# Folding a feature map into projection weights in 64 by 64 tiles on two PSUM banks, with later row statistics held back

## The chip, the core and the metric

The kernel runs on one core of a Trainium2 chip. The metric is the device time of one execution in microseconds (us); the engines are named as in the profile: PE (TensorE, the matrix engine), PEld (its weight loads), DVE (VectorE), ACT (ScalarE), POOL (GpSimd) and SP (SyncE, which issues the DMAs).

## What is computed

Two layers, each an attention block with a learned feature map and a dense block with the Mish activation, over x of 2048 rows by 640 columns, in float32, 32 heads of 20 columns:

```
def _A_ref(x, wqkv, w_phi, wo):
    q, k, v = split into heads of (x @ wqkv)                  # 32 heads, 20 wide
    pq = einsum("bhsd,hdf->bhsf", q, w_phi)                   # a 20 x 20 map for each head
    pk = einsum("bhsd,hdf->bhsf", k, w_phi)
    phi_q = concat([softmax(pq), softmax(-pq)], axis=-1)      # 40 wide
    phi_k = concat([softmax(pk), softmax(-pk)], axis=-1)
    kv, z = phi_k^T v, sum of phi_k over the rows
    o = (phi_q kv) / (phi_q z + 1e-6)
    return o @ wo
def _B_ref(x, w1, b1, w2):
    h = x @ w1 + b1
    return (h * tanh(softplus(h))) @ w2
for _ in range(2):
    x = x + _A_ref(layernorm(x), ...)
    x = x + _B_ref(layernorm(x), ...)
```

## The kernel before

The 2048 rows are worked through in eight blocks of 256 (two tiles of 128). Every large matmul is done in three parts for precision: each operand is split into a high part (rounded to the fp32r format, an ACT copy) and a low part (what is left, a DVE or POOL subtraction), and high x high, high x low and low x high are added up in PSUM.

`w_phi` isn't applied to q and k. Before the first projection it is multiplied into the query and key columns of `wqkv` ("folded"): the weights come in transposed (`wqk_t`), in raw tiles of rows of that transpose, and a matmul of a raw tile (stationary, 128 columns for one k, the index of 128 input features of 640) with the block-diagonal `phi_bd` (moving) gives folded weights for some heads, straight in the layout that the projections use. Of each head's 20 outputs only 19 are made: `shift_phi` (POOL) first subtracts the last column from the others, since a softmax doesn't change when its input is shifted, so there are 608 folded columns. `fold_part` issues one matmul, `fold_end` evicts a finished part from PSUM into a high part (ACT, L275) and a low part (DVE, L276).

Before the change the raw tiles t = 0 to 3 hold 120 rows (6 heads), and t = 4 and 5 hold 80 (4 heads). For each k there are six matmuls, three into one bank (342 columns) and three into another (266 columns), and two evictions.

The first stage of layer 0 (`attend_first` with `first is None`) is written in an order of its own (`with written()`): loads of x, `phi_bd` and the raw tiles; the first block's layer-norm statistics (L295, L297, L304, L305, L307); the query weights' fold of t = 0 to 2 for all k (`pcs`), with the first normalized rows and their transposition (L325, L331) in between; half of the first query projection (`q0[0]`, L391); then for each k the rest of the query fold and `make_v(k - 1)`, which splits one piece of the value weights (L142 on ACT, L143 on DVE); then the other half `q0[1]`. Everything behind it, the key weights' fold (`fold_phi(kv_ws, ...)`), the other projections, `features` (L407 to L427: the two softmaxes of a query or key tile `r` or `big`: copy out of PSUM, L416 maximum and minimum, L417 and L419 subtractions, exponential, L425 row sums, L426 reciprocal, L427 product; L472 turns a query tile around) and the statistics of the next blocks (`fetch_normed`), is put in order by a scheduler which works with its own time estimates: each engine gets a fixed list of instructions and works through it strictly in order, waiting on semaphores. All DMAs here are issued by SP, also in a fixed order, with at most eight outstanding. The folded query and key weights are stored to DRAM for the second layer (L222, L223).

PSUM has eight banks here: two tiles `mm` of two banks each, and four tiles `one` of one bank. The x tiles have two buffers, so that a block's x is loaded (L432) when the block two before it has been normalized (L134, `xn`).

Of the kernel before, what the change touches and what calls it, by code (L numbers as in the profile page):

```python
# [8 lines left out]
F32 = mybir.dt.float32  # L9
F32R = mybir.dt.float32r  # L10
AF = mybir.ActivationFunctionType
ALU = mybir.AluOpType
# [4 lines left out]
P = 128  # L17
S = 2048
D = 640
F = 1536  # L20
H = 32
DH = 20
DL = DH - 1
KD = D // P
KF = F // P
BT = 2
# [5 lines left out]
QK = H * DL  # L32
# [12 lines left out]
def kernel(  # L45
# [13 lines left out]
    nc = tc.nc  # L59
# [3 lines left out]
    wts = ctx.enter_context(tc.tile_pool(name="wts", bufs=1))  # L63
# [50 lines left out]
    x1_d = dram.tile([S, D], F32, name="x1_d")  # L114
    x2_d = dram.tile([S, D], F32, name="x2_d")

    last_act, in_written, last_low, last_load = [None], [False], [None], [None]

    @contextmanager
    def written():  # L120
# [19 lines left out]

    def split(hi, lo, st):
        nc.scalar.activation(hi, st, AF.Copy)  # L142
        nc.vector.tensor_tensor(lo, st, hi.bitcast(F32), op=ALU.subtract)  # L143

    def r1_spare(tag):
        return wts.tile([P, F], F32, tag=tag, name="raw1")
# [26 lines left out]
    def r2_wide(j, dtype=F32R):  # L173
        return wts.tile([P, 2, D], dtype, tag=f"r2{j}", name=f"r2{j}")
# [66 lines left out]
    def load_raw(which, ts=range(6)):  # L241

        raw = []
        for t in ts:
            rows = 120 if t < 4 else 80
            if t < 5:
                r = wts.tile([P, D], F32, tag=f"r2{'hl'[which]}{5 + t}", name=f"raw{which}{t}")
            else:
                r = r2_wide(10 + which, F32)[:, 0]

            n = P if t < 5 else rows
            c0 = which * D + (t * 120 if t < 5 else D - rows)
            nc.sync.dma_start(r[:n], wqk_t[c0:c0 + n, :])
            raw.append((r, rows))
        return raw

    def fold_part(ps, k, t, bd, raw):

        r, rows = raw[t]
        heads = rows // DH  # L260
        n = DL * (6 * (t % 3) if t < 5 else 10)
        nc.tensor.matmul(ps[:, n:n + heads * DL].rearrange("p (j d) -> p j d", d=DL), r[:rows, k * P:(k + 1) * P],
                         bd[:rows, t, :rows].rearrange("p (j d) -> p j d", d=DH)[:, :, :DL], start=True, stop=True)

    def shift_phi(bd, ts):

        b = bd[:, ts].rearrange("p t (j d) -> p (t j) d", d=DH) if isinstance(ts, slice) else (
            bd[:80, ts, :80].rearrange("p (j d) -> p j d", d=DH))
        nc.gpsimd.tensor_tensor(b[:, :, :DL], b[:, :, :DL], b[:, :, DL:].to_broadcast([b.shape[0], b.shape[1], DL]),
                                op=ALU.subtract)  # L270

    def fold_end(ws, ps, k, c):
        n0, n1 = (0, 18 * DL) if c == 0 else (18 * DL, QK)
        hi, lo = ws[k][0][:, n0:n1], ws[k][1][:, n0:n1]
        nc.scalar.activation(hi, ps[:, :n1 - n0], AF.Copy)  # L275
        nc.vector.tensor_tensor(lo, ps[:, :n1 - n0], hi.bitcast(F32), op=ALU.subtract)  # L276

    def fold_phi(ws, bd, raw):

        pss = {}  # L280
        for k, c in ((0, 0), (1, 0), (2, 0), (3, 0), (0, 1), (1, 1), (2, 1), (3, 1), (4, 0), (4, 1)):
            if c == 0:
                mm = None if k % 2 else mm_tile()
                pss[k] = [one_tile(), one_tile()] if k % 2 else [mm[:, 0], mm[:, 1]]
            ps = pss[k][c]
            for t in range(3 * c, 3 * c + 3):
                fold_part(ps, k, t, bd, raw)
            fold_end(ws, ps, k, c)


    def norm_stats(t, xt):

        bn = work.tile([P, 2, 6], F32, tag="bn", name="bn", bufs=2)
        for c in range(2):
            nc.vector.bn_stats(bn[:, c], xt[:, t, c * HC:(c + 1) * HC])  # L295
        mv = work.tile([P, 2], F32, tag="mv", name="mv", bufs=3)
        nc.vector.bn_aggr(mv, bn)  # L297
# [137 lines left out]
    def attend_first(layer, x_src, first):  # L435


        def fetch_normed(b):
            if layer:
                return load_turned(n2_d[b], [row_tile] * 3, nc.gpsimd)  # L440
            xt = fetch(x_src, b) if b > 1 else early
            norm_scale(b, [norm_stats(t, xt) for t in range(BT)])
            return xt

        pending = []
# [48 lines left out]
        if first is None:  # L494
            with written():
                xt = fetch(x_src, 0)
                bd = big_tile()[:120, :720].rearrange("p (t c) -> p t c", t=6)
                nc.sync.dma_start(bd[:, :3], phi_bd[:, :3])
                raw_q = load_raw(0, range(3))

                nc.vector.memset(bd[:80, 5, :80], 0.0)
                nc.sync.dma_start(bd[:40, 5, :40], phi_bd[80:120, 4, 80:120])
                nc.sync.dma_start(bd[40:80, 5, 40:80], phi_bd[:40, 5, :40])
                nc.sync.dma_start(bd[:, 3:5], phi_bd[:, 3:5])
# [8 lines left out]
                shift_phi(bd, slice(3, 5))  # L513
                shift_phi(bd, 5)

                q_ws = [r2_pair(k) for k in range(KD)]
                mm = [mm_tile(), mm_tile()]
                pcs = [mm[0][:, 0], mm[0][:, 1], mm[1][:, 0], mm[1][:, 1], one_tile()]
                for t in range(3):
                    for k in range(KD - 1):  # L520
                        fold_part(pcs[k], k, t, bd, raw_q)
                fold_end(q_ws, pcs[0], 0, 0)
# [4 lines left out]
                fold_end(q_ws, pcs[1], 1, 0)  # L527
                fold_end(q_ws, pcs[2], 2, 0)
                nxt = Transposed(xn)
                nxt.step()  # L530
                fold_end(q_ws, pcs[3], 3, 0)
                nxt.step()
                for t in range(3):
                    fold_part(pcs[4], 4, t, bd, raw_q)
                nxt.step()
                fold_end(q_ws, pcs[4], 4, 0)
# [474 lines left out]
```

## Time and profile before

| | us |
|---|---|
| median of 3 runs | 1365.76 |
| lowest and highest of them | 1362.42, 1367.02 |
| profiled execution, its own time | 1364.93 |
| span of that execution in the profile | 1363.0 |
| PE busy in it | 1351.1 (99%) |
| DVE, ACT, POOL busy | 1057.4, 574.7, 463.9 |

The profile is of one execution. In rows of the timeline the columns are start, duration, engine, line of the kernel, operation, output tile <- input tiles, partitions x elements, count, and in brackets the idle time of the engine ahead of it with what ended that. In rows of windows each engine has its busy time and in brackets the number of instructions; PEclk is the TensorE clock that was granted, as a share of full speed. A matmul in float32 stands as two rows (two passes) in the trace. Line numbers are those of the kernel before, also where the changed kernel is spoken of.

### The profile page before, as it was taken

Reading aid. Unit: us, or ns where it says so; the run is one execution under the profiler, and the core shown is the slowest. Engines: PE = TensorE matmul, PEld = TensorE weight load, DVE = VectorE, ACT = ScalarE, POOL = GpSimd, SP = SyncE. Lnnn points to the kernel's source line nnn. Section 1 sums busy time; section 2 is a strip of 40 time slices with the busy share of each in tenths; the row PEclk is TensorE's granted clock in tenths of the full one; section 3 lists DMA queues with packets and bytes.
Section 4 is the critical chain, followed back from the end, with each engine's and each line's share of the span. In section 5 each row is a group of like instructions: output and inputs, shape, how many; then the busy total and the mean of one; then the engine's idle time right before and its main releaser. Section 6 shows DMA issues by size and latency. Waiting matters only on the chain.

```text
span 1363.0 us, 30965 instructions
## 1 busy us (share of the span) xinstructions
PE 1351.1 (99%) x12896; PEld 1339.1 (98%) x12896; DVE 1057.4 (78%) x1801; ACT 574.7 (42%) x965; POOL 463.9 (34%) x417
## 2 busy tenths in 40 slices
PE   9999999999999999999999999999999999999998
PEld 9999999999999999999999999999999999999998
DVE  5888988876687887778769788788668777676775
ACT  4444344322454545445443334332236444444443
POOL 2355544444222222222226556634251211111111
PEclk9999999999999999999999999999999999999999
DMA  9543443798714442334463534468964221233200
GB/s 340 155 101 80 96 99 78 206 278 280 222 39 98 116 117 69 62 104 109 140 205 83 116 79 97 91 153 249 282 250 130 78 77 31 88 97 97 73 25 20
DMA packets 352629, 174.11 MB, mean 128 GB/s; under 512 B 287449, under 2 KB 324041, under 8 KB 352489
## 3 DMA queue, kind: packets, MB, share of 16 engines
q1 hardware_dynamic: 352489, 172.14, 46.3%
q8 instruction: 101, 1.65, 0.5%
q14 instruction: 39, 0.32, 0.1%
HBM read 106.23 MB, written 65.86 MB: 126 GB/s over the span
## 4 chain that ended last, share of the span: by engine, by line
PE 90%; DVE 3%; POOL 2%; DMA 1%; ACT 1%; issue 1%; SPq 0%; DVEq 0%; POOLq 0%; ACTq 0%
PE mm L839 25%; PE one L797 25%; PE mm L391 24%; PE one L391 10%; PE mm L675 2%; PE one L325 2%; PE one L464 1%; DMA raw<-in_w 1%; POOL big L427 1%; DVE r L425 1%; DVE m L416 1%; DVE r L419 1%; POOL r1l L164 1%; DVE big L417 0%; DMA e_d<-r 0%
## 5 line engine op out<-in xcount | busy, mean ns | idle before, releaser
L839 PE MATMUL mm<-r2h,ol 128*128 128x320 f32 x1280 | 304.9, 309 | 0.0
L823 POOL TENSOR_TENSOR ol<-big,ol 128x512 fp32r<-128x512 f32 (+1 forms) x98 | 131.0, 1337 | 477.8 <-ACT ol L822 419.6
L797 PE MATMUL one<-xtl,r1h 128*128 128x256 f32 x960 | 268.2, 279 | 0.0
L797 PE MATMUL one<-xth,r1l 128*128 128x256 f32 x960 | 268.0, 279 | 0.0
L797 PE MATMUL one<-xth,r1h 128*128 128x256 f32 x960 | 265.8, 279 | 0.0
L839 PEld LDWEIGHTS mm<-r2h,ol 128*128 128x128 f32 x1280 | 219.2, 188 | 0.0
L839 PE MATMUL mm<-r2l,ol 128*128 128x320 f32 x640 | 197.3, 309 | 0.0
L391 PE MATMUL mm<-r1h,xth 128*128 128x304 f32 (+1 forms) x600 | 185.2, 309 | 0.0
L391 PE MATMUL mm<-r1l,xth 128*128 128x304 f32 (+1 forms) x600 | 183.8, 306 | 0.0
L391 PE MATMUL mm<-r1h,xtl 128*128 128x304 f32 (+1 forms) x600 | 183.5, 306 | 0.2 <-POOL xtl L331 0.2
L797 PEld LDWEIGHTS one<-xtl,r1h 128*128 128x128 f32 x960 | 180.5, 188 | 0.0
L797 PEld LDWEIGHTS one<-xth,r1l 128*128 128x128 f32 x960 | 180.4, 188 | 0.0
L797 PEld LDWEIGHTS one<-xth,r1h 128*128 128x128 f32 x960 | 179.6, 188 | 0.0
L812 DVE TENSOR_SCALAR big<-big 128x512 f32<-128x512 f32 (+1 forms) x98 | 56.9, 581 | 110.3 <-ACT big L810 110.1
L839 PEld LDWEIGHTS mm<-r2l,ol 128*128 128x128 f32 x640 | 120.2, 188 | 0.0
L814 ACT ACTIVATE big<-big,two 128x512 f32<-128x512 f32 (+1 forms) x98 | 70.1, 715 | 116.2 <-DVE big L813 116.1
L822 ACT ACTIVATE ol<-big 128x512 fp32r<-128x512 f32 (+1 forms) x98 | 60.9, 622 | 137.8 <-DVE big L821 137.7
L810 ACT ACTIVATE big<-one,b1s 128x256 f32<-128x256 f32 x192 | 80.8, 467 | 89.0 <-PE one L797 88.4
L427 POOL TENSOR_TENSOR r<-r,r 128x1280 f32<-128x1280 f32 x32 | 77.2, 2411 | 117.3 <-DVE r L426 104.8
L391 PEld LDWEIGHTS mm<-r1h,xth 128*128 128x128 f32 x600 | 112.8, 188 | 1.1 <-DVE r1l L276 0.2
L391 PEld LDWEIGHTS mm<-r1h,xtl 128*128 128x128 f32 x600 | 112.8, 188 | 0.4 <-POOL xtl L331 0.4
L391 PEld LDWEIGHTS mm<-r1l,xth 128*128 128x128 f32 x600 | 112.8, 188 | 0.1
(141 smaller groups left out, 3118.7 us busy)
## 6 DMA issues: line engine op xcount, KB each, us to landing
e_d<-r SPq DMA_DIRECT2D x128, 160.0 KB, 4.0
big<-e_d SPq DMA_DIRECT2D x32, 640.0 KB, 7.1
x_d<-xt SPq DMA_DIRECT2D x23, 640.0 KB, 3.9
xt<-x_d SPq DMA_DIRECT2D x22, 640.0 KB, 5.3
n_d<-xn SPq DMA_DIRECT2D x168, 80.0 KB, 2.3
xt<-in_x SPq DMA_DIRECT2D x16, 640.0 KB, 4.6
xn<-x_d SPq DMA_DIRECT2D x28, 320.0 KB, 4.3
v<-n_d SPq DMA_DIRECT2D x30, 256.0 KB, 3.1
```

Source lines behind the costliest of these rows:

```text
L164: low.tensor_tensor(w[1][:, cs], st, w[0][:, cs].bitcast(F32), op=ALU.subtract)
L325: nc.tensor.transpose(ps[:, c, t * P:(t + 1) * P], self.rows[t][:, (c0 + c) * P:(c0 + c + 1) * P], ident)
L391: nc.tensor.matmul(ps[:, :w], a[:, sl], r, start=(k == 0 and n == 0), stop=(k == KD - 1 and n == 2))
L427: nc.gpsimd.tensor_tensor(eg, eg, r.unsqueeze(2).to_broadcast([P, 2 * H, DH]), op=ALU.mult)
L675: nc.tensor.matmul(po[64 * q:64 * q + 64, c, GW * j:GW * j + w], phs[g][:n, s0:s0 + 64], kvb[:n, g, :w], start=True, stop=True)
L797: nc.tensor.matmul(ph[:, j, :], l, r, start=(n == 0), stop=(n == 3 * KD - 1))
L810: exps[0] = nc.scalar.activation(part(ta, 0)[:, j - js.start], ph[:, j, :], AF.Exp, bias=b1s[:, 2 * pr + j:2 * pr + j + 1]).ins
L812: nc.vector.tensor_scalar_min(e, e, E_CAP)
L814: nc.scalar.activation(r, n, AF.Ln, bias=two)
L822: nc.scalar.activation(ah[:, js], n, AF.Copy)
L823: nc.gpsimd.tensor_tensor(al[:, js], n, ah[:, js].bitcast(F32), op=ALU.subtract)
L839: nc.tensor.matmul(pys[t][:, c, :HC], l[:, j, sl], r, start=(f == 0 and n == 0), stop=(f == KF - 1 and n == 2))
```

## The change

The raw tiles overlap: each holds 124 rows of which two stretches of 60 (3 heads each) begin at partitions 4 and 64; tile 0 of the query weights gets 4 rows of zeros ahead, and t = 5 is 64 rows with 2 heads. All of `phi_bd` comes in three transfers into a zeroed tile. A fold matmul now takes 64 rows (60 of them with heads) and 64 stationary columns and gives 57 columns (3 heads; 38 for t = 5): four for each tile and k, rows 0 to 63 into one bank (`ps[0]`), rows 64 to 123 into another (`ps[1]`), each in two column halves. `pair_banks` gives the two banks, either two tiles `one` or one tile `mm`. `fold_end` evicts a pair of banks in one instruction where it is one `mm` tile, in two where it is two `one` tiles, and the 38 columns of t = 5 in an instruction of their own. `fold_phi` works through k one after the other with all of t, in place of two halves. The statistics of the later blocks in layer 0 are issued no sooner than the last `split` (`issue_after(last_split[0])`).

```
     def split(hi, lo, st):
         nc.scalar.activation(hi, st, AF.Copy)
-        nc.vector.tensor_tensor(lo, st, hi.bitcast(F32), op=ALU.subtract)
+        last_split[0] = nc.vector.tensor_tensor(lo, st, hi.bitcast(F32), op=ALU.subtract).ins
...
+    def load_phi(bd):
+        nc.vector.memset(bd, 0.0)
+        for s in range(2):
+            nc.sync.dma_start(bd[4 + 60 * s:64 + 60 * s, :5], phi_bd[60 * s:60 * s + 60, :5, 60 * s:60 * s + 60])
+        nc.sync.dma_start(bd[24:64, 5, :40], phi_bd[:40, 5, :40])
...
+    def pair_banks(single):
+        if single:
+            return [one_tile(), one_tile()]
+        mm = mm_tile()
+        return [mm[:, 0], mm[:, 1], mm]
+
+    def fold_part(ps, k, t, t0, bd, raw):
+        n = 3 * (t - t0) * DL
+        heads = 3 if t < 5 else 2
+        for s in range(2 if t < 5 else 1):
+            rows = slice(64 * s, 64 if s == 0 else 124)
+            rhs = bd[rows, t, :heads * DH].rearrange("p (j d) -> p j d", d=DH)[:, :, :DL]
+            for q in range(2):
+                nc.tensor.matmul(ps[s][64 * q:64 * q + 64, n:n + heads * DL].rearrange("p (j d) -> p j d", d=DL),
+                                 raw[t][rows, k * P + 64 * q:k * P + 64 * q + 64], rhs, start=True, stop=True)
+
+    def fold_end(ws, ps, k, t0, t1):
+        n = min(t1, 5) - t0
+        w = 3 * DL
+        c0 = 2 * t0 * w
...
+        srcs = ([ps[2][:, :, :n * w].rearrange("p s (t d) -> p s t d", t=n)] if len(ps) > 2 else
+                [p[:, :n * w].rearrange("p (t d) -> p t d", t=n) for p in ps])
+        outs = list(zip(srcs, parts(ws[k][0]), parts(ws[k][1])))
+        if t1 > 5:
+            outs.append((ps[0][:, n * w:n * w + 2 * DL], ws[k][0][:, 10 * w:QK], ws[k][1][:, 10 * w:QK]))
+        for src, hi, lo in outs:
+            nc.scalar.activation(hi, src, AF.Copy)
+            nc.vector.tensor_tensor(lo, src, hi.bitcast(F32), op=ALU.subtract)
 
     def fold_phi(ws, bd, raw):
-        pss = {}
-        for k, c in ((0, 0), (1, 0), (2, 0), (3, 0), (0, 1), (1, 1), (2, 1), (3, 1), (4, 0), (4, 1)):
...
+        for k in range(KD):
+            ps = pair_banks(k % 2)
+            for t in range(6):
+                fold_part(ps, k, t, 0, bd, raw)
+            fold_end(ws, ps, k, 0, 6)
...
             xt = fetch(x_src, b) if b > 1 else early
-            norm_scale(b, [norm_stats(t, xt) for t in range(BT)])
+            with tc.issue_after(last_split[0]):
+                norm_scale(b, [norm_stats(t, xt) for t in range(BT)])
             return xt
...
                 q_ws = [r2_pair(k) for k in range(KD)]
-                mm = [mm_tile(), mm_tile()]
-                pcs = [mm[0][:, 0], mm[0][:, 1], mm[1][:, 0], mm[1][:, 1], one_tile()]
+                pcs = [pair_banks(k < 2) for k in range(KD - 1)]
...
                 for k in range(KD):
-                    ps = one_tile()
+                    ps = pair_banks(k % 2 == 0)
                     for t in range(3, 6):
-                        fold_part(ps, k, t, bd, raw_q)
-                    fold_end(q_ws, ps, k, 1)
+                        fold_part(ps, k, t, 3, bd, raw_q)
+                    fold_end(q_ws, ps, k, 3, 6)
                     if k > 0:
                         make_v(k - 1)
```

More of the change, by code (lines that the diff above doesn't have):

```diff
@@ L115 @@
     x2_d = dram.tile([S, D], F32, name="x2_d")
-    last_act, in_written, last_low, last_load = [None], [False], [None], [None]
+    last_act, in_written, last_low, last_load, last_split = [None], [False], [None], [None], [None]
     @contextmanager
@@ L244, in load_raw @@
         for t in ts:
[L245 to L254, printed above, removed]
-        return raw
[L257 to L263, printed above, removed]
+            r = (wts.tile([P, D], F32, tag=f"r2{'hl'[which]}{5 + t}", name=f"raw{which}{t}") if t < 5 else
+                 r2_wide(10 + which, F32)[:, 0])
@@ new lines, in load_raw @@
+            p0 = 4 if which == t == 0 else 0
+            n = P if t < 5 else 64
+            c0 = which * D + (120 * t - 4 if t < 5 else D - 64)
+            if p0:
+                nc.vector.memset(r[:p0], 0.0)
+            nc.sync.dma_start(r[p0:n], wqk_t[c0 + p0:c0 + n, :])
+            raw.append(r)
+        return raw
+    def load_phi(bd):
[3 more added lines that the diff above has]
+        nc.sync.dma_start(bd[24:64, 5, :40], phi_bd[:40, 5, :40])
@@ L265, in shift_phi @@
     def shift_phi(bd, ts):
[L267 to L269 removed]
+        b = bd[:, ts].rearrange("p t (j d) -> p (t j) d", d=DH)
+        nc.gpsimd.tensor_tensor(b[:, :, :DL], b[:, :, :DL], b[:, :, DL:].to_broadcast([P, b.shape[1], DL]),
                                 op=ALU.subtract)
[L272 to L276, printed above, removed]
@@ L278, in fold_phi @@
-    def fold_phi(ws, bd, raw):
-        pss = {}
-        for k, c in ((0, 0), (1, 0), (2, 0), (3, 0), (0, 1), (1, 1), (2, 1), (3, 1), (4, 0), (4, 1)):
[L282 to L288, printed above, removed]
+    def pair_banks(single):
[3 more added lines that the diff above has]
+        return [mm[:, 0], mm[:, 1], mm]
@@ new lines, in fold_end, with parts @@
+    def fold_end(ws, ps, k, t0, t1):
+        n = min(t1, 5) - t0
+        w = 3 * DL
+        c0 = 2 * t0 * w
+        def parts(x):
+            x = x[:, c0:c0 + 2 * n * w].rearrange("p (t s d) -> p s t d", t=n, s=2)
+            return [x] if len(ps) > 2 else [x[:, 0], x[:, 1]]
+        srcs = ([ps[2][:, :, :n * w].rearrange("p s (t d) -> p s t d", t=n)] if len(ps) > 2 else
[6 more added lines that the diff above has]
+            nc.vector.tensor_tensor(lo, src, hi.bitcast(F32), op=ALU.subtract)
@@ L496, in attend_first @@
                 xt = fetch(x_src, 0)
-                bd = big_tile()[:120, :720].rearrange("p (t c) -> p t c", t=6)
-                nc.sync.dma_start(bd[:, :3], phi_bd[:, :3])
+                bd = big_tile()[:, :360].rearrange("p (t c) -> p t c", t=6)
+                load_phi(bd)
                 raw_q = load_raw(0, range(3))
[L501 to L504, printed above, removed]
                 shift_phi(bd, slice(0, 3))
@@ L512, in attend_first @@
                 norm_scale(0, mvs)
-                shift_phi(bd, slice(3, 5))
-                shift_phi(bd, 5)
+                shift_phi(bd, slice(3, 6))
                 q_ws = [r2_pair(k) for k in range(KD)]
-                mm = [mm_tile(), mm_tile()]
-                pcs = [mm[0][:, 0], mm[0][:, 1], mm[1][:, 0], mm[1][:, 1], one_tile()]
+                pcs = [pair_banks(k < 2) for k in range(KD - 1)]
                 for t in range(3):
                     for k in range(KD - 1):
-                        fold_part(pcs[k], k, t, bd, raw_q)
-                fold_end(q_ws, pcs[0], 0, 0)
+                        fold_part(pcs[k], k, t, 0, bd, raw_q)
+                fold_end(q_ws, pcs[0], 0, 0, 3)
                 xn = [row_tile() for _ in range(BT)]
@@ L526, in attend_first @@
                                         op0=ALU.mult, op1=ALU.add)
-                fold_end(q_ws, pcs[1], 1, 0)
-                fold_end(q_ws, pcs[2], 2, 0)
+                fold_end(q_ws, pcs[1], 1, 0, 3)
+                fold_end(q_ws, pcs[2], 2, 0, 3)
                 nxt = Transposed(xn)
                 nxt.step()
-                fold_end(q_ws, pcs[3], 3, 0)
+                fold_end(q_ws, pcs[3], 3, 0, 3)
                 nxt.step()
+                ps = pair_banks(True)
                 for t in range(3):
-                    fold_part(pcs[4], 4, t, bd, raw_q)
+                    fold_part(ps, 4, t, 0, bd, raw_q)
                 nxt.step()
-                fold_end(q_ws, pcs[4], 4, 0)
+                fold_end(q_ws, ps, 4, 0, 3)
                 mm = mm_tile()
```

## The prediction

> **What bounds the kernel now.** I read the page first, then the chain of waits up to 45 us, since the order of TensorE's instructions in the changed program differs from before only up to about there: from the second half of the first key projection on, both programs issue the same matmuls. So one number decides: when TensorE gets through the first half of that projection (15 matmuls on `mm<-r1h`).
>
> ```profile
> span 1363.0 us, 30965 instructions
> PE 1351.1 (99%) x12896; PEld 1339.1 (98%) x12896; DVE 1057.4 (78%) x1801; ACT 574.7 (42%) x965; POOL 463.9 (34%) x417
> PE 90%; DVE 3%; POOL 2%; DMA 1%; ACT 1%; issue 1%; SPq 0%; DVEq 0%; POOLq 0%; ACTq 0%
> ```
> ```profile
> 28.21 0.79 DVE bn L295 x2
> 29.18 1.74 ACT xn L134 x2
> 30.91 0.76 ACT v L134 x3
> 31.67 1.17 ACT r L134
> 32.86 1.49 DVE r L425
> 34.35 0.85 DVE r1l L276 x2
> 35.24 0.92 PE mm L262 x6
> 42.09 2.98 PE mm L391 x21
> ```
>
> The page says TensorE, 99% busy; a delay ahead of 42 us is therefore carried to the end one for one. The chain says that ahead of 42 us it isn't TensorE that binds, but a string through DVE and ACT: statistics (L295), normalized rows (L134 xn), evicted values, the exponential of the first query tile, its row sums (L425), and only then the low parts of the folded key weights (L276), for which TensorE waits at 35.24. A faster fold is worth only what this string gives away.
>
> ```profile
> core 0: us, PE busy (x) PEld busy (x) DVE busy (x) ACT busy (x) POOL busy (x), PEclk, DMA share, GB/s
> 32.56:35.97 3.41, 2.50 (x23) 2.35 (x22) 3.11 (x6) 2.21 (x7) 0.00 (x0) 1.00 0.82 307
> 35.97:39.38 3.41, 3.41 (x19) 3.19 (x18) 3.34 (x10) 1.45 (x3) 2.36 (x1) 0.50 1.01 375
> ```
>
> These two windows show what TensorE's idling costs: after 3.41 us with 0.9 idle, the granted clock is 0.50 for the next 3.41 us.
>
> **The fold's matmuls.** Each matmul is two passes in the trace.
>
> ```profile
> 30.86 0.83 PE L262 MATMUL mm<-big,raw 120*128 120x114 f32 x6
> 31.52 0.83 PE L262 MATMUL one<-big,raw 120*128 120x114 f32 x6
> 36.81 1.47 PE L262 MATMUL mm<-big,raw 120*128 120x114 f32 x6
> 38.07 1.47 PE L325 MATMUL one<-ident,xn 128*128 128x128 f32 x6
> 39.38 0.41 PE L391 MATMUL mm<-r1h,xth 128*128 128x304 f32 x1
> 42.11 0.30 PE L391 MATMUL mm<-r1h,xtl 128*128 128x304 f32 x1
> 252.90 1.38 PE L675 MATMUL mm<-kvb,big 120*64 120x63 f32 x40
> 254.12 0.27 PE L675 MATMUL mm<-kvb,ol 80*64 80x42 f32 x4
> 254.21 1.36 PE L675 MATMUL mm<-kvb,big 120*64 120x63 f32 x40
> L464 PE MATMUL one<-big,v 128*21 128x40 f32 x2048 | 24.7, 203 | 0.5 <-POOL big L427 0.4
> 129.69 4.20 PE mm L391 x30
> ```
>
> Before: six passes from 30.86 to 31.52 are 0.11 us each; the fold has 60 matmuls, 120 passes, 13.2 us. After: per k 22 matmuls of 64 columns, so 110 for each of the two weights, 440 passes. No row has a 64 x 64 tile. The nearest above is L675, 64 columns in pairs: 44 passes from 252.90 to 254.21, 30 ns each, so 13.2 us and no gain. Below is L464, narrow tiles four at a time: 24.7 us / 2048, 12 ns, 5.3 us. I take 20 ns: 8.8 us, 4.4 us less work on TensorE. It is worth nothing as long as TensorE waits. The Trainium skill says the same against this change (TensorEngine Tiling (Array Packing), PSUM Bottleneck: tiling speeds TensorE up but not the emptying of PSUM, which may become the limit); by that rule alone the gain is nil, and the sum below is worse than nil.
>
> **Evictions: a new handshake.** Where a weight is in two banks, ACT and DVE each take two pieces; and the last 38 columns are a piece of their own (t = 5), so 1 + 1 instructions become 2 + 2 or 3 + 3. In the changed program's order, with the waits resolved, ACT's 38-column piece waits for DVE's subtraction on the same bank, and DVE's 38-column piece for ACT's. Queued behind them, in order, are ACT's `r1h` (L142) and DVE's `r1l` (L143) of the value weights, for which the value projections wait.
>
> ```profile
> 16.12 0.39 ACT L275 ACTIVATE r2h<-one 128x266 fp32r<-128x266 f32 x1 [2.29 <-PE one L262]
> 17.98 0.74 ACT L142 ACTIVATE r1h<-xn 128x640 fp32r<-128x640 f32 x1
> 20.00 0.81 DVE L143 TENSOR_TENSOR r1l<-v,r1h 128x640 fp32r<-128x640 f32 x1
> 20.74 0.42 DVE L276 TENSOR_TENSOR r2l<-one,r2h 128x266 fp32r<-128x266 f32 x1
> 21.08 0.81 DVE L143 TENSOR_TENSOR r1l<-v,r1h 128x640 fp32r<-128x640 f32 x1
> 21.81 0.81 DVE L143 TENSOR_TENSOR r1l<-big,r1h 128x640 fp32r<-128x640 f32 x1
> ```
>
> On DVE 640 columns take 0.74 from start to start (20.00 to 20.74), 266 take 0.34: 1.07 ns a column and 0.06 fixed. So 570 columns take 0.66, 285 0.36, 38 0.10, and the extra pieces alone some 1 us over the whole stage. The handshake costs more: one k is now DVE's r1l 0.74, its first eviction 0.26 to the end, ACT's short piece 0.13 with hand-over, ACT's r1h 0.74 and a hand-over 0.04: 1.9 us in place of 0.34 + 0.74 = 1.08. Let ACT start this stage at 15.7 in place of 16.12: fewer bytes of weights are loaded ahead of it, but x still comes first, and two of the first five evictions are split; 15.5 to 16.7 is possible. Ahead of the first r1l lie the evictions of k = 0 and 1 with their handshakes, 0.8 and 0.9, and r1h, 0.74: it starts at 18.2, the next at 20.1, 22.0, 24.0 and, without an eviction between, 24.8; the last one ends at 25.6, where before it ends at 22.62 (21.81 + 0.81).
>
> **The statistics, held back and moved ahead of the key weights.** The diff issues the later blocks' statistics no sooner than the last such subtraction. In the order, DVE then has both next blocks' statistics (8 of L295, not 6) before the query tile's L416, and the third block's ones directly after L425, ahead of all evictions of the folded key weights; before, these came first and that block's statistics stood behind them, at 37.38.
>
> ```profile
> 24.07 1.67 DVE L295 BATCH_NORM_STATS2 bn<-xt 128x6 f32<-128x320 f32 x4 [1.01 <-DMA xt<-in_x]
> 25.66 0.33 DVE L297 BATCH_NORM_AGGREGATE mv<-bn 128x2 f32<-128x12 f32 x2
> 26.69 1.53 DVE L416 TENSOR_REDUCE m<-r 128x32 f32<-128x640 f32 x2
> 27.57 1.28 POOL L417 TENSOR_TENSOR r<-r,m 128x640 f32<-128x640 f32 x1 [0.39 <-DVE m L416]
> 30.94 0.33 SPq L432 DMA_DIRECT2D xt<-in_x  x1
> 36.21 0.54 DVE L426 RECIPROCAL r<-r 128x64 f32<-128x64 f32 x1
> 37.38 1.60 DVE L295 BATCH_NORM_STATS2 bn<-xt 128x6 f32<-128x320 f32 x4
> 40.45 1.46 DVE L472 STREAM_TRANSPOSE r<-r 128x1280 f32<-128x1280 f32 x1
> ```
>
> From 25.6: four L295 are 1.6 (24.07 to 25.66), two L297 0.25, four more 1.6, both L416 1.45, statistics 0.25: ACT's xn starts at 30.8 in place of 29.18. From there ACT's part is as in the chain, 3.68 us from 29.18 to L425 at 32.86: L425 at 34.5. (POOL's L417 starts after the first L416, at 29.8, and is done at 31.1, well ahead.) L425 gives DVE free at 35.9.
>
> Now DVE waits for the third block's x. Its load waits on SP for xn, so it is issued at about 32.5, not 30.94. It can't land before 34.2 (640 KB at the window's near 395 GB/s are 1.7 us), nor later than 38.9 (before, the statistics found it landed 6.4 us after the issue). I take 36.1, near the low end, because what is queued ahead of it, the ten stores of query weights, is the same as before and drains whenever this load is issued. Queued behind this wait on DVE: every key-weight eviction, the reciprocal for which POOL waits, the transposition.
>
> From 36.1: two L295 0.8, r1l0 0.66, two L295 0.8, L426 0.5, r1l1 2 x 0.36, two L297 with r1l0's short piece 0.3: 39.85, when the bank pair is free into which k = 4 is folded. Until then TensorE, which ends the value projections at 31.1 (25.7 + 38 matmuls of 4.20 / 30 = 0.14) and the other folds at about 34.8, stands idle for 5 us. Then DVE has r1l2 0.66, a memset 0.3, four pieces of r1l1 to r1l3 0.9, the transposition 1.4, a piece and statistics 0.3, r1l4 0.66: 44.1.
>
> **The sum.** TensorE after 39.85, at half clock (by the rows at 36.81, 38.07 and 39.38, six transposes take 1.31, 0.22 each; a matmul 0.28): fold of k = 4, 44 passes of 40 ns, 1.8; four transposes 0.9; 12 matmuls 3.4; six transposes 1.3; 3 matmuls 0.8: 8.2 us, so 48.05 if all of it is slow. The clock returns at a time T, one window of 3.41 us after the first full one of work: between 43.3 and 46.7. The end is (48.05 + T) / 2, 45.7 to 47.4, in the middle 46.5. Before it was 42.25 (42.11 + 0.14). That is +3.4 to +5.1, middle +4.3 us.
>
> The profiled execution of before took 1364.93 us, 1.93 more than its span and 0.83 less than the median of 1365.76. So the profile after should have a span near 1367.3, and the median 1370.1. The runs before spread from 1362.42 to 1367.02, and about 0.3%, 4.1 us, is what can be told from no change: the forecast stands just beyond it.
>
> **Rivals.** First: the clock doesn't drop, or comes back by 41. Then DVE's 44.1 binds, two matmuls more make 44.45, +2.2: 1368.0. For it: 3.41 us windows need not fall into the gap. Against: in the row a mere 0.9 us of idling did it, and here 5 us are idle, so I give it 0.17. The Trainium skill (TensorE: Matmul & The Clock Gate, Part 1) has the clock halved after about one whole idle window of 3.4 us, free-running. By that rule before should have kept its clock, which the row contradicts; here 5 us hold a whole window about half the time, and this case would be as likely as mine.
>
> Second: the 64 x 64 passes don't overlap at all. Then each takes half of 0.11, 55 ns, for half the columns; 172 passes from 31.1 are 9.5 us, to 40.6, and the rest at full clock (TensorE never idles) 2.4 + 0.5 + 1.7 + 0.8 + 0.4: 46.4, +4.2, 1370.0. L675's 30 ns speak against it. 0.12.
>
> Third, faster: DVE keeps pace, and TensorE alone decides. Before lost 0.9 us idle and, at half clock, 0.6 on six passes and 1.1 on ten transposes; the key weights' fold falls from 60 x 0.11 = 6.6 to 220 x 0.02 = 4.4. Together -4.8: 1361.0. It decides this way if r1l4 is ready by 37.2; I get 44.1, as DVE's order is fixed, and even at before's own times the third block's wait precedes the evictions. 0.07.
>
> **How the numbers follow.** My case has 0.64, of which 0.43 is beyond 4.1 us (two thirds of its range, and x landing later adds up to 2.8 us) and 0.21 within. With the first rival (0.17 within), the second (0.07 slower, 0.05 within) and the third (0.07): slower 0.50, same 0.43, faster 0.07. Without the third, 2.2 us at the least, less 1.6 (a third of the 4.6 over which the runs spread), gives 1366.3; the other end is +5.1 with x landing 2.8 us late and something for the median, 1374.
>
> **What would show it.** Right: L143's last subtraction ends near 25.6; an L295 waits for DMA between L425 and the first low part of the key weights; TensorE idles some 5 us ahead of the fold of k = 4; a window of clock 0.50 after it, into which the first key matmuls fall; from then on the same distances as before. Wrong: fold passes at 50 ns and more with no idle gap (second rival), the first key projection ahead of 42 us (third), or a difference that arises behind 50 us, where nothing is moved on TensorE.

## The result and the profile after

| | before | after |
|---|---|---|
| median | 1364.10 us (5 runs, 1362.42 to 1367.02) | 1375.89 us (5 runs, 1375.77 to 1376.54) |
| profiled execution, its own time / span | 1364.93 / 1363.0 | 1375.89 / 1374.0 |
| end of the first half of the first key projection | 42.25 | 54.25 |

The changed kernel is slower, by a ratio of 1.0088 (95% interval 1.0077 to 1.0100), 11.8 us. The forecast of 1370.1 had the direction; 1375.9 lies outside its range of 1366.3 to 1374.0.

In the changed kernel the lines have other numbers: L284 is the fold's matmul (L262 before), L303 and L304 its high and low evictions (L275, L276), L319 the statistics (L295), L415 the projections (L391), L440 and L449 the maximum and the row sums (L416, L425), L456 the load of x (L432). Kernels with further edits shift these by one to four. "Third block" is used as in the prediction, for the third of the later blocks, the one whose x waits for `xn`. Everywhere else ("the second block", "the blocks after the second", "the fourth block", and the expectation of the last run) the count is from the first block of all, so that the blocks after the second are the second and third of the later blocks and all behind them.

The page of the changed kernel:

```profile
span 1374.0 us, 31634 instructions
PE 1350.4 (98%) x13216; PEld 1336.9 (97%) x13216; DVE 1062.7 (77%) x1815; ACT 576.7 (42%) x978; POOL 463.6 (34%) x416
```

TensorE is as busy as before (1351.1) in a span 11.0 us longer: the time is idle time and half clock, not work. Where, the timeline of its engines shows (start, duration, engine, line, operation, tiles, shape, and in brackets the idle time before it and what ended that):

```profile
2.62 2.65 SPq L252 DMA_DIRECT2D raw<-in_wqk_t  x5
5.97 1.05 SPq L185 DMA_DIRECT2D xn<-in_wv  x2
11.61 1.57 SPq L185 DMA_DIRECT2D v<-in_wv  x2
11.73 0.69 PE L284 MATMUL one<-big,raw 64*64 64x57 f32 x16 [4.93 <-DMA raw<-in_wqk_t]
21.73 0.42 ACT L303 ACTIVATE r2h<-one 128x114 fp32r<-128x114 f32 x2 [1.85 <-PE one L284]
30.71 0.82 DVE L143 TENSOR_TENSOR r1l<-big,r1h 128x640 fp32r<-128x640 f32 x1
37.06 1.74 ACT L134 ACTIVATE xn<-xt,stats 128x640 f32<-128x640 f32 x2 [3.55 <-DVE stats L331]
40.74 1.49 DVE L449 TENSOR_REDUCE r<-r 128x64 f32<-128x1280 f32 x1 [1.70 <-ACT r L134]
43.99 0.89 DVE L319 BATCH_NORM_STATS2 bn<-xt 128x6 f32<-128x320 f32 x2 [1.76 <-DMA xt<-in_x]
47.76 1.33 PE L284 MATMUL mm<-big,raw 64*64 64x57 f32 x40 [7.36 <-DVE mv L321]
51.20 0.74 DVE L304 TENSOR_TENSOR r1l<-mm,r1h 128x570 fp32r<-128x570 f32 x1
54.11 0.30 PE L415 MATMUL mm<-r1h,xtl 128*128 128x304 f32 x1
```

The first fold matmul starts at 11.73; before, the corresponding one started at 6.56:

```profile
6.56 1.08 PE L262 MATMUL mm<-big,raw 120*128 120x114 f32 x8
```

TensorE waits 4.93 us for the first raw tile, and SP itself stands still from 7.0 to 11.61, so that everything issued behind is late too. From there the forecast's chain follows, link by link, some 6 us behind the forecast's times, and some 8 us from the third block's x on: statistics, `xn`, row sums, DVE's wait for that x, TensorE idle for 7.36 us ahead of the fold of k = 4. The windows of the changed kernel show the clock (the columns are as in the prediction):

```profile
9.00:12.00 3.00, 0.27 (x10) 0.30 (x13) 0.00 (x0) 0.00 (x0) 0.00 (x0) 0.50 1.05 219
41.83:45.24 3.41, 0.00 (x0) 0.00 (x0) 1.65 (x4) 0.02 (x1) 0.00 (x0) 0.66 0.05 21
48.66:52.10 3.44, 3.44 (x34) 3.36 (x28) 3.44 (x11) 1.62 (x5) 1.87 (x6) 0.50 1.00 371
```

Half clock stands twice here, once because of the late raw tile; in the trace's clock records it lasts from 8.82 to 19.06 and from 42.95 to 53.19 us, three windows of 3.41 us each time, where the kernel before has one (35.97 to 39.38). At the end of the first key half-projection the changed kernel is 12.0 us behind, and at its end 11.0 us by the spans: on balance the loss is complete by then. (TensorE's instructions matched one by one, it is 13.3 us behind at 320 us of the kernel before, and gets some 2 us back at 921, where the kernel before waits 1.8 us and the changed one does not.)

### The profile page after: what moved, and what is told of

Read it like the earlier page. It is cut to its first block, busy times and chain, and to the rows that moved or that the text cites. A ratio compares the mean times of both kernels' runs of the same rounds, so it can differ in the third digit from the quotient of the medians.

```text
span 1374.0 us, 31634 instructions
## 1 busy us (share of the span) xinstructions
PE 1350.4 (98%) x13216; PEld 1336.9 (97%) x13216; DVE 1062.7 (77%) x1815; ACT 576.7 (42%) x978; POOL 463.6 (34%) x416
## 4 chain that ended last, share of the span: by engine, by line
PE 82%; DVE 5%; POOL 2%; DMA 1%; issue 1%; ACT 0%; SPq 0%; DVEq 0%; POOLq 0%; ACTq 0%
PE mm L858 25%; PE one L816 24%; PE mm L415 16%; PE one L415 11%; PE mm L694 3%; PE one L349 2%; DVE r L449 1%; PE one L489 1%; DVE m L440 1%; DVE r L497 1%; DMA e_d<-r 1%; DVE r L443 1%; DMA raw<-in_w 1%; POOL r L451 1%; DVE big L441 1%; POOL big L451 1%
## 5 line engine op out<-in xcount | busy, mean ns | idle before, releaser
L415 PE MATMUL mm<-r1h,xth 128*128 128x304 f32 (+1 forms) x600 | 186.0, 310 | 0.5 <-ACT r L134 0.5
L415 PE MATMUL mm<-r1h,xtl 128*128 128x304 f32 (+1 forms) x600 | 184.1, 307 | 0.2 <-POOL xtl L355 0.2
L415 PE MATMUL mm<-r1l,xth 128*128 128x304 f32 (+1 forms) x600 | 184.3, 307 | 0.0
L415 PEld LDWEIGHTS mm<-r1h,xth 128*128 128x128 f32 x600 | 113.4, 189 | 1.6 <-ACT r L134 0.7
L415 PEld LDWEIGHTS mm<-r1h,xtl 128*128 128x128 f32 x600 | 113.3, 189 | 0.4 <-POOL xtl L355 0.4
L415 PEld LDWEIGHTS mm<-r1l,xth 128*128 128x128 f32 x600 | 113.4, 189 | 0.1
```

The source lines that it names most:

```text
L415: nc.tensor.matmul(ps[:, :w], a[:, sl], r, start=(k == 0 and n == 0), stop=(k == KD - 1 and n == 2))
```

## The experiments

Theory: the late first raw tile, a transfer of 124 rows, is the part that the forecast lacked, and the rest is the forecast's chain. The rivals are that later waits set the end anyhow, and that the handshake or the held-back statistics carry more than was put on them. Times are medians; the ratio is to the kernel before on the same chip. That kernel's own median differs from chip to chip by up to 0.8 us, so that rows with different values there are best compared by what each lies above it. The last column is read from the one profiled execution, whose time lies up to 3.7 us from its row's median.

| edit (to the kernel after, except where named) | us | before, same chip | ratio, 95% interval | half-projection ends |
|---|---|---|---|---|
| 120 rows | 1370.28 | 1364.69 | 1.0043 (1.0030 to 1.0057) | 49.23 |
| kernel before with 124 rows | 1371.18 | 1364.69 | 1.0048 (1.0035 to 1.0060) | 48.39 |
| high parts first | 1375.44 | 1364.69 | 1.0079 (1.0065 to 1.0092) | 52.56 |
| statistics not held | 1382.42 | 1364.69 | 1.0133 (1.0118 to 1.0149) | 61.24 |
| 120 rows, statistics not held | 1380.49 | 1364.18 | 1.0122 (1.0105 to 1.0140) | 58.38 |
| 120 rows, high parts first | 1371.03 | 1364.18 | 1.0050 (1.0038 to 1.0063) | 48.69 |
| 120 rows, later statistics behind k = 3 | 1368.82 | 1364.18 | 1.0032 (1.0020 to 1.0045) | 46.10 |
| both of these edits | 1368.63 | 1364.18 | 1.0027 (1.0017 to 1.0038) | 44.23 |
| 120 rows, high first, behind k = 4 | 1367.36 | 1363.93 | 1.0025 (1.0015 to 1.0036) | 41.42 |
| 120 rows, behind k = 4 | 1368.53 | 1363.93 | 1.0033 (1.0021 to 1.0044) | 46.35 |
| kernel before, statistics behind k = 4 | 1362.59 | 1363.93 | 0.9990 (0.9981 to 0.9999) | 39.67 |
| 120 rows, high first, only from the fourth block on behind k = 4 | 1365.87 | 1364.43 | 1.0011 (1.0002 to 1.0020) | 42.73 |

**The first raw tile in 120 rows.**

```
             p0 = 4 if which == t == 0 else 0
-            n = P if t < 5 else 64
+            n = 124 if p0 else P if t < 5 else 64
             nc.sync.dma_start(r[p0:n], wqk_t[c0 + p0:c0 + n, :])
```

> The changed kernel, with one edit: the first raw tile of the query weights is loaded in 120 rows (partitions 4 to 123) in place of 124; the four rows left out are not read by the fold. Transfer theory: the 124 rows go out on 4 transfer engines only (the trace shows 4 completions, 11.0 to 11.6 us, for 16 of every other tile), 31 rows each, so the tile lands at 11.6 where before it landed at 6.4, and the 5.2 us are carried to the end, since everything up to the first key projection hangs on that fold. With 120 rows on 15 engines it lands at about 6.5, the first fold matmul stands at 6.6 in place of 11.73, and the median falls by 5 to 6 us from 1375.9, to 1370 to 1371, the forecast's value. Rival, later waits: handshake and third block's x set the end whenever the front end starts; then the fold starts earlier but the median stays within 1.5 us of 1375.9.

1370.28 us, 5.6 us less, by four rows that nothing reads; above the kernel before of the same chip 5.6 us are left of the 11.8. The timeline of this kernel:

```profile
7.77 0.46 PE L284 MATMUL one<-big,raw 64*64 64x57 f32 x16 [1.52 <-DMA raw<-in_wqk_t]
16.11 0.42 ACT L303 ACTIVATE r2h<-one 128x114 fp32r<-128x114 f32 x2 [1.79 <-PE one L284]
18.50 0.83 DVE L143 TENSOR_TENSOR r1l<-xn,r1h 128x640 fp32r<-128x640 f32 x1 [0.43 <-DMA raw<-in_wqk_t]
20.41 0.83 DVE L143 TENSOR_TENSOR r1l<-xn,r1h 128x640 fp32r<-128x640 f32 x1 [0.43 <-ACT r1h L142]
25.09 0.82 DVE L143 TENSOR_TENSOR r1l<-big,r1h 128x640 fp32r<-128x640 f32 x1
31.43 1.74 ACT L134 ACTIVATE xn<-xt,stats 128x640 f32<-128x640 f32 x2 [3.55 <-DVE stats L331]
32.35 0.77 PE L284 MATMUL one<-big,raw 64*64 64x57 f32 x40
33.05 0.77 PE L284 MATMUL mm<-big,raw 64*64 64x57 f32 x38
35.12 1.49 DVE L449 TENSOR_REDUCE r<-r 128x64 f32<-128x1280 f32 x1 [1.70 <-ACT r L134]
38.58 0.49 DVE L319 BATCH_NORM_STATS2 bn<-xt 128x6 f32<-128x320 f32 x1 [1.98 <-DMA xt<-in_x]
42.28 1.33 PE L284 MATMUL mm<-big,raw 64*64 64x57 f32 x40 [7.51 <-DVE mv L321]
```

and two of its windows:

```profile
45.24:48.66 3.42, 3.42 (x16) 3.39 (x15) 2.00 (x7) 0.46 (x2) 0.12 (x2) 0.50 0.99 314
48.66:52.10 3.44, 3.44 (x27) 3.44 (x26) 0.00 (x0) 0.57 (x1) 0.00 (x0) 1.00 0.85 182
```

This is the kernel that the forecast describes. The transfer theory holds; the fold starts at 7.77 and not at 6.6, for the most part as two more transfers of `phi_bd` now stand ahead of the tile on SP (it is issued at 2.62, before at 1.67).

**The kernel before with 124 rows** in its first raw tile:

```
+            if which == t == 0:
+                n = 124
             nc.sync.dma_start(r[:n], wqk_t[c0:c0 + n, :])
```

> The kernel before, in which only the first raw tile of the query weights is loaded in 124 rows in place of 128 (its fold reads 120). Transfer theory: it goes out on 4 transfer engines, lands at 10 to 11.5 us in place of 6.4, and the median rises by 4 to 5.5 us, to 1368 to 1369.5. Rival: the first fold has slack in this kernel, and the median stays within 1 us of 1364.1.

1371.18, 6.5 us more and above the expectation; the first key half-projection ends 6.1 us later than before. The longest of TensorE's waits, and a window behind it, show the transfer and a cost that the theory had not counted:

```profile
PE mm L264 <- DMA raw<-in_wqk_t: 4.4, 1, 4.4
12.00:16.00 4.00, 4.00 (x19) 4.00 (x20) 0.00 (x0) 0.00 (x0) 1.06 (x5) 0.50 0.85 244
```

The wait also drops the clock, so the fold's first matmuls behind it run at half speed. The transfer alone, without any other part of the change, makes the kernel before as slow as the changed kernel is with 120 rows.

**High parts first.**

```
         for src, hi, lo in outs:
             nc.scalar.activation(hi, src, AF.Copy)
+        for src, hi, lo in outs:
             nc.vector.tensor_tensor(lo, src, hi.bitcast(F32), op=ALU.subtract)
```

> The changed kernel with the evictions of one weight tile in another order: all pieces of the high part first, then all subtractions, so that the scalar engine's short piece waits for no subtraction. Handshake theory: a weight tile's cycle falls from the 1.9 to 2.0 us seen to 1.2 to 1.4, the last value-weight subtraction ends some 3 us earlier than 31.5, and the median falls by 2.5 to 3.5 us, to 1372.5 to 1373.5. Rival: that stage has slack, as the folds of tiles 3 to 5 and the raw value weights arrive late; the median moves by less than 1 us.

Only 0.4 us (1.0 by what each kernel lies above the kernel before of its chip), and the intervals of the two ratios overlap. The handshake itself did go, as its timeline shows:

```profile
27.50 0.82 DVE L143 TENSOR_TENSOR r1l<-big,r1h 128x640 fp32r<-128x640 f32 x1
39.79 1.67 DVE L320 BATCH_NORM_STATS2 bn<-xt 128x6 f32<-128x320 f32 x4 [3.95 <-DMA xt<-in_x]
41.38 1.47 DVE L450 TENSOR_REDUCE r<-r 128x64 f32<-128x1280 f32 x1
49.02 0.88 DVE L305 TENSOR_TENSOR r1l<-one,r1h 128x285 fp32r<-128x285 f32 x3
49.82 0.84 DVE L305 TENSOR_TENSOR r1l<-mm,r1h 128x570 fp32r<-128x570 f32 x2
```

The last subtraction of the value weights ends at 28.3, 3.2 us ahead of 31.5. But the scheduler now put the third block's statistics ahead of the row sums (L450), and DVE waits 3.95 us for that x: row sums, which started at 40.74, start at 41.38, and the last low part, at 51.20, starts at 49.82. Neither theory had this; the 3 us are real, and are spent in the next wait. With 120 rows as well:

> The changed kernel with both edits: the first raw tile in 120 rows, and all high parts of a weight tile ahead of its subtractions. Handshake theory, corrected by the run with the second edit alone (there the value weights were done 3.2 us earlier, but the third block's statistics then stood ahead of the row sums, and the median fell by 0.4 us only): the last value-weight subtraction ends near 22.7 in place of 25.9, and the median falls by 1 us at most below the 1370.3 of the run with 120 rows, to 1369 to 1370. Rival, plain addition on the path: the 3.2 us are carried to the end: 1367.

1371.03: no gain either, for the same reason.

```profile
35.91 1.67 DVE L320 BATCH_NORM_STATS2 bn<-xt 128x6 f32<-128x320 f32 x4 [4.38 <-DMA xt<-in_x]
37.50 1.47 DVE L450 TENSOR_REDUCE r<-r 128x64 f32<-128x1280 f32 x1
```

**Statistics not held back** (`issue_after(last_split[0])` taken out), in the changed kernel and with 120 rows:

> The changed kernel without the issuing order that holds the later blocks' statistics behind the last subtraction of the value weights. Order theory: 5.2 us of statistics no longer stand between the last value-weight subtraction (31.5) and the normalized rows (37.1), they run where the vector engine waits in the handshakes; the third block's load, the exponential and the key-weight evictions come 2 to 4 us earlier: 1372 to 1374. Rival: the statistics only push the handshakes back by what they save, and the third block's statistics stand ahead of the row sums anyway: 1375 to 1377.

> The changed kernel with the first raw tile in 120 rows, without the order that holds the later blocks' statistics back. Hold-pays theory: the vector engine then has the second block's statistics ahead of the evictions of the second fold stage and waits for that block's x, which lands at 24.5: the stage starts some 6 us late, 1375 to 1377. Rival: with the front end mended x is there in time, and the hold costs what the prediction put on it (1.6 us more of statistics between value weights and normalized rows): 1368 to 1370.

1382.42 and 1380.49: the hold is no cost here, it saves 6.5 and 10.2 us. The order theory of the first expectation is wrong; the hold-pays theory of the second has the mechanism, but 1380.49 lies 3.5 us above its range, as the first subtraction of the value weights stands at 29.43 in place of 18.50, later by 10.9 us and not by some 6. Without the hold the scheduler puts the second block's statistics ahead of the second fold stage's evictions, where its x isn't there yet (timeline of the kernel with 120 rows):

```profile
24.07 1.67 DVE L319 BATCH_NORM_STATS2 bn<-xt 128x6 f32<-128x320 f32 x4 [9.47 <-DMA xt<-in_x]
```

**The later statistics further back.** With 120 rows, the statistics of the blocks after the second are issued no sooner than a low part of the key weights, that of k = 3 (as here) or of k = 4 (`KD - 1`); `fold_end` returns its last subtraction. This moves the second of the later blocks too: DVE then has four statistics and not eight ahead of the row sums.

```
-            fold_end(ws, ps, k, 0, 6)
+            low = fold_end(ws, ps, k, 0, 6)
+            if k == KD - 2:
+                last_split[0] = low
```

> The changed kernel with the first raw tile in 120 rows, and with the statistics of the blocks after the second issued no sooner than the last low part of key-weight tile k = 3. Order theory: the vector engine no longer waits at 36.6 to 38.6 for the third block's x, nor has four statistics in between; the bank pair for k = 4 comes free at about 38.7 in place of 42.3, the clock comes back one window of 3.41 us earlier, and the median falls by 3 to 3.6 us below 1370.3, to 1366.7 to 1367.3. Rival: the statistics and the wait only change places and then hold back the low part of k = 4, whose matmuls close the first key half-projection: within 1 us of 1370.3.

> The changed kernel with all three edits: 120 rows, high parts first, later statistics behind the low part of k = 3. Order theory: the 3.2 us of the handshake now reach the end as well: value-weight subtractions end near 22.7, the pair for k = 4 is free near 35.5, the matrix engine idles 2 to 3 us in place of 7.5: 1363 to 1365, level with the kernel before, or below it if the clock drops for one window only. Rival, transfers: the stores of the query weights and the third block's x bind instead: 1366 to 1367.

1368.82 and 1368.63: below the run with 120 rows alone by 1.5 and 1.7 us, less than the order theory had and with intervals that overlap; the rival is half right. The second also compares with the run with 120 rows and high parts first on the same chip, 2.4 us above it, where the intervals just touch. In the first of the two:

```profile
37.22 0.94 PE L284 MATMUL mm<-big,raw 64*64 64x57 f32 x40 [2.79 <-DVE r1l L304]
44.93 0.74 DVE L304 TENSOR_TENSOR r1l<-mm,r1h 128x570 fp32r<-128x570 f32 x1
```

The pair for k = 4 came free at 37.2 in place of 42.3, TensorE's idle time fell from 7.51 to 2.79; but the low part of k = 4 now stands behind eight statistics. In the second, with the high parts first, that costs 3.01 us of idling and another window of half clock (timeline and windows of that kernel):

```profile
43.85 0.41 PE L419 MATMUL mm<-r1l,xth 128*128 128x304 f32 x1 [3.01 <-DVE r1l L305]
41.31:44.72 3.41, 0.87 (x6) 0.88 (x7) 3.26 (x12) 0.00 (x0) 1.24 (x5) 1.00 0.89 159
44.72:48.13 3.41, 3.41 (x16) 3.41 (x15) 0.23 (x2) 0.28 (x1) 1.24 (x4) 0.50 0.92 253
```

So they were held behind k = 4 too:

> The changed kernel with 120 rows, high parts first, and the statistics of the blocks after the second issued no sooner than the last low part of the last key-weight tile (k = 4, in place of k = 3). Order theory: in the run with k = 3 the low part of k = 4 stood behind eight statistics, ended at 43.9, and the matrix engine idled 3.0 us at 43.85, with a second slow window after it. Without that the low part is done near 40, the half-projection ends near 40.5 to 41 in place of 44.2, and the median falls by 3 to 5 us below 1368.6: 1363.5 to 1365.5, level with the kernel before. Rival: what is late after 45 us (the scales of the later blocks, the query features) sets the end whatever the half-projection does: 1367.5 to 1369.

> The same with the evictions in the changed kernel's own order (120 rows, statistics behind the last low part of k = 4). Handshake theory: the value weights end 3.2 us later than with the high parts first, but the second block's x lands only at 23.9, so that 1.7 us of it remain: 1365 to 1367, 1.5 us above the run with the high parts first. Rival, the handshake is hidden: within 0.7 us of that run.

> The kernel before, in which the statistics of the later blocks are issued no sooner than the last low part of the last key-weight tile. Order theory: the four statistics at 37.4 to 38.9 leave the way of the low part of k = 4, the matrix engine idles less by up to 1 us: 1363 to 1364. Rival: no change, as the matrix engine is busy there: 1364 to 1364.5; if the statistics are then too late for the third block, above 1365.

1367.36 with the high parts first and 1368.53 without: 1.2 us for the handshake once the statistics are out of its way, with overlapping intervals, though the half-projection ends 4.9 us apart (41.42 and 46.35). The first key half-projection now ends at 41.42, ahead of before's 42.25, and still the kernel is 3.4 us slower, 0.1 us below the rival's range: it was right that the half-projection doesn't set this end. The longest of TensorE's waits between 42 and 360 us (in the kernel before, the longest there is 0.4 us):

```profile
PE one L419 <- DVE xt L728: 1.2, 1, 1.2
PE mm L419 <- DVE xtl L359: 0.7, 1, 0.7
PE mm L419 <- ACT r L134: 0.6, 1, 0.6
```

Only the second of them, at 54.8 us, comes where the rival looked for late scales and low parts. The first and third stand at 323.6 and 144.5, in instructions that the edits didn't touch; the changed kernel waits at the same two places (0.6 and 0.5 us), the kernel before at neither. TensorE's instructions matched one by one, this kernel is 0.9 us ahead of the kernel before at the half-projection, and behind it by 1.1 at 84 us of the kernel before, by 2.1 at 142 and by 3.7 at 320 (by 1.4 at the end of this execution, 1366.32, the fastest of its eight). Why the late waits arise isn't shown.

The same hold in the kernel before gave 1362.59, 1.3 us less and 0.4 below the range of its theory: the interval just leaves out 1. This is the fastest version of all, and has nothing of the fold's change in it. The last run holds back only what lies further off (`last_split[-1]` is the last low part of k = 4):

```
-            with tc.issue_after(last_split[0]):
+            with tc.issue_after(last_split[0 if b < 3 else -1]):
```

> The changed kernel with 120 rows and high parts first, in which only the statistics of the blocks from the fourth on are held behind the last low part of k = 4; those of the second and third keep the changed kernel's place, behind the value weights. In the run that held the third block's too, the first key half-projection ended at 41.4, 0.8 us before the kernel before, and yet the median was 3.4 us above it; the matrix engine waited 2.5 us behind 42 us for what comes out of late scales and low parts. Theory: the third block's late statistics are what was lost there; they now cost 1.8 us ahead of the row sums and save the 2.5 us: 1365.5 to 1366.7. Rival: the loss behind 42 us is not theirs, and the 1.8 us only add to it: 1368.5 to 1369.5.

1365.87, as the theory had it. Its trace doesn't confirm the mechanism, however: the waits for `xt` and `r` behind 42 us are still there (1.0 and 0.8), and the profiled execution was the slowest of its eleven, 1368.21. Where this run saved time against the one with all of them behind k = 4 stays open.

Another comparison is clearer. This run differs from the one with 120 rows and high parts first only in the place of the statistics of the third block and those behind it, and it lies 1.4 us above the kernel before of its chip, where that one lies 6.9 above; the intervals are well apart. The fold of k = 4 in that run, and in this one:

```profile
39.96 1.33 PE L284 MATMUL mm<-big,raw 64*64 64x57 f32 x40 [7.05 <-DVE mv L322]
36.15 0.81 PE L284 MATMUL mm<-big,raw 64*64 64x57 f32 x40 [2.74 <-DVE r1l L305]
```

DVE no longer stands 4.38 us in front of that block's x, the half-projection ends at 42.73 and not at 48.69, and half clock lasts one window and not four.

## Why the prediction was wrong, point by point

**The step that failed** is the front end: "Let ACT start this stage at 15.7 in place of 16.12: fewer bytes of weights are loaded ahead of it ...; 15.5 to 16.7 is possible". It was 21.73, 6.0 us late. The bytes were counted, and not the rows: the first raw tile is one transfer of 124 rows, where before it had 128 (the other tiles of 124 used rows still load 128). In the trace's completion records (increments of the load's semaphore) it has 4 completions, from 10.99 to 11.60 us; the 128-row load of before has 16, the last one at 6.39; the 120-row load has 15, the last one at 7.63. So 310 KB went out through a quarter of the transfer engines, and what was queued behind them there landed late as well: of the next raw tile, 12 completions came by 7.15 us, and the other 4 from 12.31 to 12.84 (before, its last came at 7.75). The Trainium skill (DMA: Bandwidth & Descriptors, section Why a DMA increments its semaphore by 16 and not by 1) says that a transfer gets the largest number of engines up to 16 that divides the outermost dimension: 4 for 124 rows, 15 for 120, 16 for 128. The traces agree with all three. The prediction had no term for this load.

**The rest of the chain held**, as the run with 120 rows shows, forecast first: ACT's start 15.7, measured 16.11; first subtraction of the value weights 18.2, 18.50; cycle 1.9, 1.91 (18.50 to 20.41); end of the last one 25.6, 25.91; `xn` 30.8, 31.43; row sums 34.5, 35.12; TensorE idle 5, 7.51.

**One more term was short.** With 120 rows x landed at 38.6 in place of 36.1, inside the stated 34.2 to 38.9, so k = 4 could be folded at 42.28 in place of 39.85. Its load was issued at 33.19 and took 5.4 us, not the 3.6 forecast; the stores queued ahead weren't what held it, as the transfer engines were busy for 0.31 of the time from 33 to 34 us and for 0.06 from 37 to 38. The clock came back at 48.66, not at 43.3 to 46.7, after three windows at half speed; but the forecast's own rule, counted from 42.28, gives 45.7 to 49.1, so this comes with the late x. The half-projection ended at 49.2, not 46.5.

That the median of 1370.28 is so near the forecast's 1370.1 is luck. The forecast counted 4.3 us on top of 1365.76, and this kernel lies 5.6 us above the 1364.69 of the same chip; and the profiled execution, from which the steps are read, was the slowest of its five, 1372.77.

**The handshake's price.** The cycle was right, but its 3 us were added to the end one for one. The two runs without it gained 0.4 us and nothing; 1.2 us, not clear of the spread, once the third block's statistics were moved. The wait for x behind it had the last word.

**The held-back statistics** were counted only as a delay. The part of them that hurt is the third block's, as the prediction said: with 120 rows and high parts first, their place alone made the difference between 6.9 and 1.4 us above the kernel before. The hold as such saves 6 to 10 us, because without it the new order would stall earlier.

**The fold.** 44 passes take 0.70 us (32.35 to 33.05), 16 ns each, below the 20 taken and inside 12 to 30. That gain stayed worthless: no version with the new fold, not even the one that ends the half-projection first, was faster than the kernel before.

**The rivals.** The clock did drop; passes overlap (16 ns, not 55); TensorE alone does not decide. Against the first rival the prediction held that "a mere 0.9 us of idling did it" in the kernel before. That kernel's trace has a second window with the same work, and behind it the clock stayed at full speed:

```profile
8.66:12.07 3.41, 2.50 (x20) 2.10 (x19) 1.86 (x4) 2.26 (x5) 1.06 (x5) 1.00 1.06 312
12.00:16.00 4.00, 4.00 (x32) 3.74 (x31) 2.64 (x6) 1.83 (x5) 0.00 (x0) 1.00 1.04 396
```

So 0.9 us of idling came before half clock once and once not; the 7.51 us of the kernel with 120 rows held a whole idle window (35.01 to 38.42), and half clock followed. The sign of being wrong that the prediction named last, a difference behind 50 us where nothing is moved, did show in the versions that end the half-projection early.

## What to carry to other kernels

Read a changed transfer by its row count and not only by its bytes: here four rows that nothing reads cost some 6 us, and the same 124 rows in the kernel before 6.5 us. When a delay in a chain is taken away, look for the next wait before adding it to the end: 3.2 us of handshake were worth 0.4 us as long as DVE stood in front of a late x, and with that wait out of the way the kernel came within 1.4 us of the kernel before. And where a scheduler fixes the order, an issue constraint that looks like a delay may be the one thing that keeps a late load out of the path.

## What the runs showed of the hardware

A transfer of 124 rows of 2,560 bytes took until 11.60 us from its issue at 2.62, one of 128 rows from 1.67 to 6.39, one of 120 rows from 2.62 to 7.63. The clock: a window in which TensorE worked for 0.87 of 3.41 us was followed by one of half clock, and in the kernel before one with 2.50 was (32.56 to 35.97), while another with 2.50 was not (8.66 to 12.07). From 5 to 60 us of the fourteen traces, windows taken as the clock records divide the time, every window at full clock with 1.39 us of work or less was followed by half clock and none with more than 2.51 was; between these two values both occur. A window of full work at half clock came before the return to full speed (45.24 to 48.66 with 120 rows, 35.97 to 39.38 in the kernel before). The Trainium skill (TensorE: Matmul & The Clock Gate, Part 1) puts the drop after a whole idle window; in these rows less was enough.
